# Splitting one unit's output product into three single-pass matmuls, with its conversion and a softmax step moved, in a chained attention and two-layer MLP kernel

## The chip, the cores and the metric

The kernel runs on one core of one Trainium2 chip. The metric is the device time of one execution in microseconds (us); the median of the runs shown is compared.

## The reference

A packed attention (32 packed queries `p` attend to `k`, `v`; then `q` attends to that packed result) gives an array of 2304 tokens by 512. It goes through two two-layer MLPs: the first with softplus, the second with SiLU (512 to 2048 to 512 each).

```python
p_packed = sm_attn(p, k, v)
out = sm_attn(q, p_packed, p_packed)
...
x = out.transpose(0, 2, 1, 3).reshape(B * S, H * D)
h = x @ w_in;  g = softplus(h);  x = g @ w_out
h = x @ w_in2; g = silu(h);      x = g @ w_out2
```

All data are float32 in size (the weights arrive as float64 words and are rebuilt on the chip).

## The kernel before, in words

**Products.** TensorE multiplies either plain float32 operands, or float32 operands that were split into a high and a low part of a type it takes in a single pass. A split product is three matmuls (low by high, high by low, high by high). Line 540 is the plain output product of the first MLP, line 547 the split one, line 501 its input product (always split; six matmuls for a chunk).

**Steps.** The first MLP and the attention are woven together by `run_steps` (line 767). A step s computes one chunk of 128 hidden features for one block of 288 tokens: the input product (`emit_in`), then softplus on ScalarE (`act_scalar`), and, for an earlier unit, one output column group dm of 128 (`emit_out`), which `finish_out` adds to or writes into the accumulator `ya`. A unit u is a set of chunks of one block. The first four units have two chunks each: u0 and u1 are chunks 0 and 1 of blocks 0 and 1 (steps 0 to 3), u2 and u3 are chunks 2 and 3 of blocks 0 and 1 (steps 4 to 7). From step 8 on a unit has four chunks (u4 is block 2, steps 8 to 11). The output products of u0 to u2 are issued two column groups at a time in steps 1 to 6; those of u3 one at a time in steps 8 to 11; step 7 has none. Before, u0 to u3 are all plain: softplus writes `gf` (line 507), and the product reads `wo_plain` (line 540). From u4 on softplus writes `gt` (513), ScalarE copies the high part `gh` (514), VectorE subtracts for the low part `gl` (`act_vector`, line 518), and line 547 multiplies.

**The order of the work is written out by hand** and every engine runs its own queue in that order. Attention pieces and weight conversions are generators (`Item`) which stop at named points: a step calls the points in the order next, D0, A0, input product, PE, `act_scalar`, `emit_out`, PE2, A1, D1, A2, `act_vector`, D, `finish_out`, D2. A generator due at the point that is called issues its next piece there. `OS` (line 763) gives for each early output weight the step of its high copy (line 176, at A0) and of its low subtraction (line 178, at D0).

**The attention pieces that lie in steps 4 to 11.** `att1(2)`: scores (330) at step 6, row maxima (336) at the end of step 6, exponentials `e0`, `e1` (342) in step 7, their transposes (351, `turn`) in step 9, copies out of PSUM (355, 358) in step 9, weighting with v (366) in step 10, normalising (391 to 394) at the end of step 10, a last transpose (399) in step 11 and its copy (403). `att2(3)` (block 3): product (414) and transpose (423) in step 5, row maxima (427, 428) at the end of step 6, exponential (430) in step 7, then "normalise" (432 to 439: sum, reciprocal, multiply, 32-square transpose) at D0 of step 8, high copy (444) and low part (446) of block 3's activations in step 8. Block 3 is first multiplied in step 12.

**Buffers.** PSUM results `h` and `y` have two banks each, the attention's `psa` two pairs. A bank is free for the product two further on only when its reader (softplus for h, `finish_out` for y) is done. `gh`/`gf` and `gl` have eight buffers each, `gt` two.

Of the kernel before, what the change touches and what calls it, by code (L numbers as in the profile page):

```python
# [18 lines left out]
B, H, S, D = 4, 8, 576, 64  # L19
# [31 lines left out]
def body(ctx, tc, kT, vv, qT, pT, wi1, wo1, wi2, wo2, out):  # L51
# [265 lines left out]
    def att1(b):  # L317

        HS = S // 2
        sm = l0.tile([P, 8], F32, name="sm", bufs=2)  # L320
        e, et, s1 = [None] * NR, [None] * NR, [None] * NR

        def scores():
            pz, kt = kts[b]
            s1[:] = two_banks(), two_banks()
            for half in range(2):
                for k in range(NK):
                    for r in range(NR):
                        rows = slice(64 * r, 64 * r + 64)
                        nc.tensor.matmul(  # L330
                            s1[r][32 * k:32 * k + 32, half, :HS], lhsT=pz[rows, k, :],
                            rhs=kt[rows, k, half * HS:(half + 1) * HS], start=True, stop=True,
                        )

        def top(r):
            nc.vector.tensor_reduce(
                out=sm[:, 2 + r:3 + r], in_=s1[r][:, :, :HS], axis=AX.XY, op=ALU.max, negate=True
            )

        def exp(r):  # L340
            e[r] = att.tile([P, S], F32, name=f"e{r}")
            nc.scalar.activation(  # L342
                out=e[r].rearrange("p (h s) -> p h s", h=2), in_=s1[r][:, :, :HS],
                func=AF.Exp, bias=sm[:, 2 + r:3 + r],
            )

        def turn(r):
            t = s1[r] = two_banks()
            for c in range(KC):
                n = min(P, S - c * P)  # L350
                nc.tensor.transpose(t[:n, c // 4, (c % 4) * P:(c % 4 + 1) * P], e[r][:, c * P:c * P + n], ident)

        def turned(r):
            et[r] = att.tile([P, KC, P], F32, name="et", bufs=2)
            nc.scalar.activation(
                out=et[r][:, :4, :], in_=s1[r][:, 0, :].rearrange("p (c f) -> p c f", c=4), func=AF.Copy
            )
            nc.scalar.activation(out=et[r][:64, 4, :], in_=s1[r][:64, 1, :P], func=AF.Copy)

        def weigh(*at):  # L360
            vt = vts[b]
            for r, c in at:
                n = min(P, S - c * P)
                for k in range(NK):
                    h = 2 * k + r
                    nc.tensor.matmul(  # L366
                        po[32 * k:32 * k + 32, r, :D1], lhsT=et[r][:n, c, 32 * k:32 * k + 32],
                        rhs=vt[:n, c, h * D1:(h + 1) * D1], start=(c == 0), stop=(c == KC - 1),
                    )

        yield "PE"
        scores()
        yield "D2" if b == 2 else "D"
        top(0)
        top(1)
        yield "A1"
        exp(0)
        exp(1)
        yield "PE"
        turn(0)  # L380
        turn(1)
        yield "A1"
        turned(0)
        turned(1)
        yield "PE2"

        po = two_banks()
        chunks = [(r, c) for r in range(NR) for c in range(KC)]
        weigh(*(sorted(chunks, key=lambda rc: rc[1] == KC - 1) if b else chunks))
        yield "D2"  # L390
        nc.vector.tensor_scalar(out=sm[:, 4:6], in0=po[:, :, D], scalar1=1e-9, scalar2=None, op0=ALU.add)
        nc.vector.reciprocal(out=sm[:, 6:8], in_=sm[:, 4:6])
        px = att.tile([P, NR, D], F32, name="px")
        nc.vector.tensor_tensor(
            out=px, in0=po[:, :, :D], in1=sm[:, 6:8].unsqueeze(2).to_broadcast([P, NR, D]), op=ALU.mult
        )
        yield "PE" if b == 1 else "PE2"
        pt_ps = two_banks()[:, 0, :P]
        nc.tensor.transpose(pt_ps, px.rearrange("p r d -> p (r d)"), ident)
        yield "A1"  # L400

        pt = pts[b] = l0.tile([P, P], F32, name="pt", bufs=B)
        nc.scalar.activation(out=pt, in_=pt_ps, func=AF.Copy)

    def att2(blk, last=False):

        b = blk // 2
        G = N0 // NP
        yield "PE"
        tq = two_banks()  # L410
        for k in range(NK):
            for r in range(NR):
                rows = slice(64 * r, 64 * r + 64)
                nc.tensor.matmul(  # L414
                    tq[32 * k:32 * k + 32, r, :N0], lhsT=pts[b][rows, k * NP:(k + 1) * NP], rhs=qts[blk][rows, k, :],
                    start=True, stop=True,
                )
        yield "D1"

        tr = att.tile([P, NR * G, NP], F32, name="tr", bufs=2)  # L420
        mx = att.tile([P, 2, NR * G], F32, name="mx", bufs=2)
        wide = [P, NR * G, NP]
        nc.vector.transpose(tr.rearrange("q (r g) p -> q r (g p)", r=NR), tq[:, :, :N0])
        if blk == 3:
            yield "next"
        yield "D2" if blk == 3 else "D"
        nc.vector.tensor_reduce(out=mx[:, 0], in_=tr, axis=AX.X, op=ALU.max)
        nc.vector.tensor_tensor(out=tr, in0=tr, in1=mx[:, 0].unsqueeze(2).to_broadcast(wide), op=ALU.subtract)
        yield "A1"
        nc.scalar.activation(out=tr, in_=tr, func=AF.Exp, scale=SCALE)  # L430
        yield "D" if blk == 2 else "D0"
        nc.vector.tensor_reduce(out=mx[:, 1], in_=tr, axis=AX.X, op=ALU.add)
        nc.vector.tensor_scalar(out=mx[:, 1], in0=mx[:, 1], scalar1=1e-9, scalar2=None, op0=ALU.add)
        nc.vector.reciprocal(out=mx[:, 1], in_=mx[:, 1])
        if blk == 2:
            yield "D2"
        nc.vector.tensor_tensor(out=tr, in0=tr, in1=mx[:, 1].unsqueeze(2).to_broadcast(wide), op=ALU.mult)
        tb = att.tile([P, NR, N0], F32, name="tb", bufs=1)
        nc.vector.transpose(tb, tr.rearrange("q (r g) p -> q r (g p)", r=NR))
        if last:  # L440
            yield "next"
        yield "A1"
        cols = slice(blk * N0, (blk + 1) * N0)
        nc.scalar.activation(out=ax[:, :NR, cols], in_=tb, func=AF.Copy)
        yield "D"
        nc.vector.tensor_tensor(
            out=ax[:, NR:, cols], in0=tb, in1=ax[:, :NR, cols].bitcast(F32), op=ALU.subtract
        )
# [53 lines left out]
        return h  # L502

    def act_scalar(s, h):
        if s < 2 * GJ:
            gf = g0.tile([P, N0], F32, name="gf", tag="gh")
            nc.scalar.activation(out=gf, in_=h, func=AF.Softplus)
            gs[steps[s]] = gf
            return None
        gt = cp.tile([P, N0], F32, name="gt")  # L510
        gh = g0.tile([P, N0], F32R, name="gh")
        gl = g0.tile([P, N0], F32R, name="gl")
        nc.scalar.activation(out=gt, in_=h, func=AF.Softplus)  # L513
        nc.scalar.activation(out=gh, in_=gt, func=AF.Copy)  # L514
        return gt, gh, gl
# [7 lines left out]
    def emit_out(s):  # L523
        u, i = steps[s]
        if s < 2 * GJ:
            if s not in AHEAD:
                return []
            u, first = AHEAD[s]
            dms = first, first + 1
        else:  # L530
            u, dms = u - 1, (i,)
        js, blk = units[u]
        n = BLOCKS[blk][1]
        ys = []
        for dm in dms:
            y = ps.tile([P, 512], F32, name="y")[:, :n]
            c = slice(dm * P, (dm + 1) * P)
            for x, j in enumerate(js):
                if len(js) < GJ:
                    nc.tensor.matmul(  # L540
                        y, lhsT=wo_plain[j][:, c], rhs=gs[u, x], start=(j == js[0]), stop=(j == js[-1])
                    )
                    continue
                gh, gl = gs[u, x]
                wh, wl = whl["o", j]
                for m, (w, g) in enumerate(((wl, gh), (wh, gl), (wh, gh))):
                    nc.tensor.matmul(  # L547
                        y, lhsT=w[:, c], rhs=g, start=(j == js[0] and m == 0), stop=(j == js[-1] and m == 2)
                    )
            ys.append((u, dm, y))  # L550
        return ys
# [152 lines left out]
    def start():  # L704
# [55 lines left out]
        for k, n, ss in ("i", 2, (1,)), ("i", 3, (2,)), ("o", 2, (3,)), ("o", 3, (4,)):  # L760
            plan(w[k, n], ss)

        OS = (3, 4), (4, 5), (5, 6), (10, 11)
        for n in range(GJ):
            plan(w["o", n], OS[n])

    def run_steps(end):
        for s in range(end):
# [19 lines left out]
            if s == 1:  # L788
                for y in ys:
                    finish_out(*y)  # L790
                    items[0].run("A1")
                ys = []
            go("A1")
            go("D1")
            go("A2")
# [633 lines left out]
```

## Time and profile before

| | us |
|---|---|
| median of 3 runs | 740.46 (740.44 to 740.78) |
| the profiled execution's own time | 740.1 |
| its span, first to last instruction | 738.3 |
| TensorE busy | 729.5 |
| VectorE busy | 564.1 |
| ScalarE busy | 388.9 |

Instructions are named by engine (PE is TensorE, PEld its weight loads, DVE VectorE, ACT ScalarE, POOL GpSimd, SP the queue that issues DMAs) and by line. A timeline row gives the start, the duration and the count of neighbouring like instructions; in brackets stands the idle time ahead of them and what ended it. Neighbours overlap a little, since a matmul's or an activation's tail runs under the next one; the spacing of starts is what one costs in a queue. A plain float32 matmul shows as two records.

### The profile page before, as it was taken

To read this page: it belongs to the slowest core of one execution; us is meant where nothing else is said; L and a number is where in the kernel's file an instruction comes from. 1 tells how busy PE (TensorE), PEld (TensorE's weight loads), DVE (VectorE), ACT (ScalarE), POOL (GpSimd) and SP (SyncE) were. 2 spreads that over 40 slices of the span, in tenths; PEclk is the share of its full clock that TensorE was granted. 3 is DMA by queue.
4 is the path that set the end of the run, shared out by engine and by line. 5 is a ranking of instruction groups with operands and counts; after the bars stand their busy time and mean duration, and the time that the engine had idled before them with its cause. 6 is when DMAs were issued, how large, how long until landed. Compare 5 with 4: busy or idle time off the path is not lost.

```text
span 738.3 us, 13860 instructions
## 1 busy us (share of the span) xinstructions
PE 729.5 (99%) x5402; PEld 698.0 (95%) x5402; DVE 564.1 (76%) x1017; ACT 388.9 (53%) x745; POOL 162.3 (22%) x140
## 2 busy tenths in 40 slices
PE   8999999999999999999999999999999999999997
PEld 7876999999999999999999999999999999999997
DVE  3888887879878897897746685767776976877667
ACT  3667886656555664566535544443353453454341
POOL 0000000000000000000000000000267999966755
PEclk9999999999999999999999999999999999999999
DMA  8965033145454362474359888789999789998942
GB/s 342 354 221 180 9 144 115 59 186 166 168 211 160 141 222 92 158 270 170 146 150 377 304 327 322 259 310 343 363 348 382 271 270 374 330 349 286 310 135 92
DMA packets 64674, 173.73 MB, mean 235 GB/s; under 512 B 5728, under 2 KB 34400, under 8 KB 61280
## 3 DMA queue, kind: packets, MB, share of 16 engines
q1 hardware_dynamic: 64608, 172.85, 65.5%
q8 instruction: 42, 0.69, 0.4%
q14 instruction: 24, 0.20, 0.1%
HBM read 136.65 MB, written 36.18 MB: 234 GB/s over the span
## 4 chain that ended last, share of the span: by engine, by line
PE 94%; ACT 3%; DVE 2%; issue 0%; POOL 0%; POOLq 0%; DVEq 0%
PE y L547 25%; PE y L1028 13%; PE h L501 13%; PE y L1140 11%; PE pA L970 7%; PE pC L970 7%; PE pB L970 7%; PE pD L970 3%; PE y L698 2%; PE psa L463 2%; PE y L540 2%; PE psa L330 1%; PE psa L366 1%; PE psa L414 1%; ACT e L342 0%
## 5 line engine op out<-in xcount | busy, mean ns | idle before, releaser
L547 PE MATMUL y<-gh,w 128*128 128x288 f32 x960 | 212.0, 296 | 0.1
L547 PEld LDWEIGHTS y<-gh,w 128*128 128x128 f32 x960 | 160.5, 188 | 12.8 <-issue 5.9
L547 PE MATMUL y<-gl,w 128*128 128x288 f32 x480 | 141.6, 295 | 0.0
L1002 POOL TENSOR_TENSOR sums<-c 128x384 f32<-128x384 f32 x13 | 15.5, 1193 | 500.6 <-ACT c L1292 500.6
L501 PE MATMUL h<-ax,vw 128*128 128x288 f32 x768 | 124.4, 297 | 0.0
L501 PEld LDWEIGHTS h<-ax,vw 128*128 128x128 f32 x768 | 108.9, 188 | 2.0 <-issue 0.5
L1028 PE MATMUL y<-G,w 128*128 128x384 f32 x480 | 93.8, 334 | 0.0
L547 PEld LDWEIGHTS y<-gl,w 128*128 128x128 f32 x480 | 90.1, 188 | 0.5 <-DVE gl L518 0.5
L1140 PE MATMUL y<-G,w 128*128 128x384 f32 x480 | 89.5, 334 | 0.0
L1028 PEld LDWEIGHTS y<-G,w 128*128 128x128 f32 x480 | 84.2, 188 | 0.0
L513 ACT ACTIVATE gt<-h 128x288 f32<-128x288 f32 x120 | 48.5, 405 | 67.0 <-PE h L501 62.3
L1140 PEld LDWEIGHTS y<-G,w 128*128 128x128 f32 x480 | 83.7, 188 | 0.0
L518 DVE TENSOR_TENSOR gl<-gt,gh 128x288 fp32r<-128x288 f32 x120 | 54.2, 452 | 25.2 <-ACT gh L514 24.4
L970 PE MATMUL pA<-xc,w 128*128 128x384 f32 x288 | 57.8, 335 | 0.1
L970 PE MATMUL pB<-xc,w 128*128 128x384 f32 x288 | 57.7, 334 | 0.0
L970 PE MATMUL pC<-xc,w 128*128 128x384 f32 x288 | 57.7, 334 | 0.0
L514 ACT ACTIVATE gh<-gt 128x288 fp32r<-128x288 f32 x120 | 53.4, 445 | 3.8
L1288 ACT ACTIVATE tc<-tc 128x384 f32<-128x384 f32 x24 | 12.6, 526 | 75.5 <-DVE tc L1188 75.4
L563 DVE TENSOR_TENSOR ya<-y,ya 128x288 f32<-128x288 f32 x104 | 46.9, 452 | 7.2 <-PE y L547 7.0
L970 PEld LDWEIGHTS pA<-xc,w 128*128 128x128 f32 x288 | 50.4, 188 | 0.4 <-ACT ta L1210 0.4
L970 PEld LDWEIGHTS pB<-xc,w 128*128 128x128 f32 x288 | 50.6, 188 | 0.0
L1010 POOL TENSOR_TENSOR G<-sums,G 128x384 fp32r<-128x384 f32 x40 | 49.0, 1248 | 7.1 <-ACT G L1006 7.1
(143 smaller groups left out, 1168.8 us busy)
## 6 DMA issues: line engine op xcount, KB each, us to landing
w<-wd SPq DMA_DIRECT2D x84, 512.0 KB, 5.9
wd<-whl SPq DMA_DIRECT2D x8, 1792.0 KB, 6.8
w<-td SPq DMA_DIRECT2D x56, 256.0 KB, 6.2
w<-od SPq DMA_DIRECT2D x42, 256.0 KB, 5.3
w<-od SPq DMA_DIRECT2D x20, 512.0 KB, 6.2
wraw<-wi SPq DMA_DIRECT2D x16, 512.0 KB, 5.6
wraw<-wo SPq DMA_DIRECT2D x16, 512.0 KB, 6.1
raw<-wi SPq DMA_DIRECT2D x16, 512.0 KB, 6.4
```

What stands on the lines that cost most here:

```text
L463: nc.tensor.matmul(t[32 * k:32 * k + 32, r, :512 if wide else 256], lhsT=pts[b][rows, k * NP:(k + 1) * NP], rhs=w[rows, :], start=True, st ...
L501: nc.tensor.matmul(h, lhsT=w, rhs=x, start=(i == 0), stop=(i == len(mm) - 1))
L513: nc.scalar.activation(out=gt, in_=h, func=AF.Softplus)
L514: nc.scalar.activation(out=gh, in_=gt, func=AF.Copy)
L518: nc.vector.tensor_tensor(out=gl, in0=gt, in1=gh.bitcast(F32), op=ALU.subtract)
L547: nc.tensor.matmul(y, lhsT=w[:, c], rhs=g, start=(j == js[0] and m == 0), stop=(j == js[-1] and m == 2))
L563: nc.vector.tensor_tensor(out=acc, in0=y, in1=acc, op=ALU.add)
L970: nc.tensor.matmul(out, lhsT=a, rhs=b, start=start and not i, stop=not start and i == len(mm) - 1, skip_group_check=True,)
L1002: eng.tensor_tensor(out=sum_of(q), in0=a, in1=b, op=op)
L1010: eng.tensor_tensor(out=u[:, 1], in0=sum_of(q), in1=u[:, 0].bitcast(F32), op=ALU.subtract)
L1028: nc.tensor.matmul(y, lhsT=w, rhs=g, start=not m, stop=m == len(mm) - 1)
L1140: nc.tensor.matmul(y, lhsT=a[:, c], rhs=G[:, g, h, j], start=(k % 2 == j == m == 0), stop=(k % 2 == j == 1 and m == 2),)
```

## The change

- The test for plain work becomes `u < 3` in place of "fewer than four chunks": u3 (block 1, chunks 2 and 3; steps 6 and 7) now writes `gt`, `gh`, `gl`, and its output products in steps 8 to 11 are split ones.
- Output weight 3 gets its high and low parts in steps 6 and 7 in place of 10 and 11.
- `att1(2)`'s transposes are issued at PE2 of step 9, behind that step's output product, in place of PE, ahead of it.
- `att2(3)`'s normalise is issued at D1 of step 7 in place of D0 of step 8.
- In step 8, `finish_out` is issued right behind PE2, ahead of A1, D1, A2 and `act_vector`.

```diff
@@ att1
-        yield "PE"
+        yield "PE2" if b == 2 else "PE"
         turn(0)
         turn(1)
@@ att2
-        yield "D" if blk == 2 else "D0"
+        yield "D" if blk == 2 else "D1" if blk == 3 else "D0"
         nc.vector.tensor_reduce(out=mx[:, 1], in_=tr, axis=AX.X, op=ALU.add)
@@ act_scalar
-        if s < 2 * GJ:
+        if steps[s][0] < 3:
             gf = g0.tile([P, N0], F32, name="gf", tag="gh")
@@ emit_out
-                if len(js) < GJ:
+                if u < 3:
                     nc.tensor.matmul(
                         y, lhsT=wo_plain[j][:, c], rhs=gs[u, x], start=(j == js[0]), stop=(j == js[-1])
                     )
@@ start
-        OS = (3, 4), (4, 5), (5, 6), (10, 11)
+        OS = (3, 4), (4, 5), (5, 6), (6, 7)
@@ run_steps
+            if s == 2 * GJ:
+                finish_out(*ys.pop())
             go("A1")
             go("D1")
             go("A2")
```

## Rows read from the trace of the kernel before

**Rows 1.** The page: its head, the granted clock of its slices, its chain by engine.

```profile
span 738.3 us, 13860 instructions
...
PEclk9999999999999999999999999999999999999999
...
PE 94%; ACT 3%; DVE 2%; issue 0%; POOL 0%; POOLq 0%; DVEq 0%
```

**Rows 2.** The chain that ended last: start, duration, what (0 to 90 us).

```profile
28.05 1.09 PE psa L351 x10
...
33.97 1.41 PE psa L366 x80
...
36.37 0.20 PE psa L399
36.58 0.60 PE psa L463 x16
...
40.11 0.65 PE psa L414 x16
...
49.68 2.14 PE y L540 x8
51.81 0.81 PE h L501 x6
...
52.65 0.41 ACT gf L507
...
62.57 0.46 DVE gl L518
...
70.33 0.67 PE psa L463 x16
```

**Rows 3.** Timeline of PE, steps 8 to 14 and one later step without attention work.

```profile
53.24 1.13 PE L540 MATMUL y<-gf,wraw 128*128 128x288 f32 x4
54.00 1.16 PE L501 MATMUL h<-ax,vw 128*128 128x288 f32 x6
55.82 1.43 PE L351 MATMUL psa<-ident,e 128*128 128x128 f32 x10 [0.66 <-ACT e L342]
...
60.42 1.24 PE L540 MATMUL y<-gf,wraw 128*128 128x288 f32 x4 [1.16 <-DVE ya L563]
...
64.89 1.04 PE L501 MATMUL h<-ax,vw 128*128 128x288 f32 x6
...
72.62 0.96 PE L501 MATMUL h<-ax,vw 128*128 128x288 f32 x6
...
99.94 0.30 PE L547 MATMUL y<-gh,w 128*128 128x288 f32 x1
...
101.52 0.96 PE L501 MATMUL h<-ax,vw 128*128 128x288 f32 x6
```

**Rows 4.** Timeline of DVE, steps 6 to 8.

```profile
50.55 0.65 DVE L178 TENSOR_TENSOR w<-wraw,w 128x512 fp32r<-128x512 f32 x1
51.38 0.76 DVE L446 TENSOR_TENSOR ax<-tb,ax 128x576 fp32r<-128x576 f32 x1 [0.18 <-ACT ax L444]
...
54.24 1.41 DVE L336 TENSOR_REDUCE sm<-psa 128x1 f32<-128x576 f32 x2
55.57 0.74 DVE L432 TENSOR_REDUCE mx<-tr 128x18 f32<-128x576 f32 x1
...
57.65 0.78 DVE L439 STREAM_TRANSPOSE tb<-tr 128x576 f32<-128x576 f32 x1
```

**Rows 5.** Timeline of ACT, steps 6 and 8.

```profile
50.66 0.68 ACT L444 ACTIVATE ax<-tb 128x576 fp32r<-128x576 f32 x1 [1.87 <-DVE tb L439]
...
58.18 0.45 ACT L514 ACTIVATE gh<-gt 128x288 fp32r<-128x288 f32 x1
```

**Rows 6.** Timeline of PE: the first matmuls, later ones of the same kind, the last.

```profile
1.34 5.49 PE L698 MATMUL y<-ident 128*128 128x128 f32 x24 [1.34 <-POOL ident masks.py:199]
...
16.40 3.39 PE L698 MATMUL y<-ident 128*128 128x128 f32 x28
...
733.66 0.68 PE L1028 MATMUL y<-tw,w 128*128 128x384 f32 x3
```

**Rows 7.** Windows behind the last matmul: busy time of PE, PEld, DVE, ACT, POOL, clock, DMA.

```profile
737.00:737.20 0.20, 0.00 (x0) 0.00 (x0) 0.00 (x0) 0.00 (x0) 0.00 (x0) 1.00 0.00 0
737.20:737.40 0.20, 0.00 (x0) 0.00 (x0) 0.00 (x0) 0.00 (x0) 0.00 (x0) 0.50 0.00 0
```

## The prediction

> **What bounds the kernel now.** I read the page first. Its chain of waits is PE for 94% of the span [rows 1], so in nearly all of the kernel a matmul saved is time saved, and a stall of PE in the early steps is carried to the end. All that the change touches lies between 47 and 68 us, so I went on to the chain there in order of time [rows 2], and it says something else: it leaves PE behind step 7's input product (the row at 51.81), runs over ACT from 52.65 and over DVE from 62.57, and comes back to PE only at 70.33. In steps 7 to 13 PE is not the bound.
>
> The timelines say where PE waits. In step 9 it waits 0.66 us for the exponentials, in step 10 it waits 1.16 us for a y bank that `finish_out` of step 8 has not freed [rows 3]. On DVE, steps 6 to 8 are one block of work with next to no holes: the low part of block 2 at 51.38 (0.18 idle ahead of it), accumulations, maxima, then the normalise of block 3 from 55.57 to 57.65 + 0.78 = 58.43 [rows 4].
>
> **The change, part by part.**
>
> *Split in place of plain products.* A column group of u3 is two products. Plain, eight records (four products) took 2.14 us, so one product is 0.535 us [rows 2]. Split, a step's twelve matmuls take 101.52 - 99.94 = 1.58 us, so one is 0.132 and a product of three 0.395 [rows 3]. Eight products save 8 x 0.14 = 1.1 us of PE.
>
> *What the split adds.* ACT gets two `gh` copies, 0.45 us each [rows 5]; DVE two `gl` subtractions, 0.46 each [rows 2]. In step 6, `gh` and the moved high copy of output weight 3 (some 0.6 us; I price it as its low half on DVE, 0.65 [rows 4]) go into ACT's 1.87 us of waiting ahead of the row at 50.66 [rows 5]: nothing. Were that cover gone, block 2's high copy would start up to 1.1 us later. In step 7, `gh` pushes ACT's exponentials back by up to 0.45; the transposes that read them are now behind more work, and it does not show. DVE's `gl` of step 6 fits partly into the 0.18 hole and pushes DVE by about 0.15 (bounds 0 and 0.46).
>
> *Weight 3's conversion in steps 6 and 7.* It issues no DMA, and no queue of SP or POOL is passed. Its low subtraction comes to lie at D0 of step 7, between the maxima and the normalise: 0.60 us by the spacing of starts, 0.65 busy [rows 4], all of it in DVE's solid block.
>
> *Normalise at D1 of step 7.* This is the term that decides. D1 comes ahead of `act_vector` in a step. Without a `gl` in step 7 the move would be nothing, since no DVE work lay between D1 of step 7 and D0 of step 8. With the split there is one: `gl` of step 7. It now queues behind the normalise, and the fifth of the six matmuls of step 8's output product reads it. Behind that matmul on PE stand the input products of steps 9, 10 and 11, all in order. So: normalise ends at 58.43 + 0.15 + 0.60 = 59.2; `gl` takes 0.46; the fifth matmul starts at about **59.65**. Step 8's first four matmuls would be done by 53.9 (start at about 53.4, as the row at 53.24, plus 4 x 0.132). PE stands idle for **about 5.7 us**, where the longest wait of these steps was 1.16.
>
> From there PE has no wait that I can find until step 14: two matmuls 0.26, then input product 0.80, output 0.79, transposes 1.09 (step 9), 0.80 + 0.79 + 1.41 (step 10), 0.80 + 0.79 + 0.20 (step 11) [rows 2, 3], 7.7 together: step 12 starts at 67.4, against 64.89 before [rows 3], 2.5 later. Steps 12 and 13 hold 2 x (0.80 + 0.65 + 0.60 + 1.58) = 7.3 us of work [rows 2, 3] and took 72.62 - 64.89 = 7.7 because DVE was late (the row at 70.33 [rows 2]); with DVE's low part of weight 3 gone from step 11 and PE later, that wait goes. Step 14 starts at 74.7 against 72.62: **+2.1 us** (bounds 1.7 and 2.5, for the 0.15 above and for waits of a few tenths). Behind it all producers are fed by PE itself and no wait of PE there is for a DMA, so it is carried to the end.
>
> *Transposes behind the output product, `finish_out` early.* Both remove waits (0.66 and 1.16 [rows 3]) that the longer one swallows; worth nothing here. `finish_out` of step 8 now stands ahead of `gl` of step 8 and of block 3's low part and waits for the stalled product itself; what is queued behind it is wanted only in steps 10 to 12. If the stall were not there, the 1.16 would go.
>
> *The clock.* The granted clock is full in every slice of the page [rows 1]. But the trace shows twice what PE does about idleness. After the last matmul (733.66 + 0.68 = 734.34 [rows 6]) the clock falls from 1.00 to 0.50 at 737.2 [rows 7], so 2.9 us later. And at the start, out of idleness, 24 matmuls take 5.49 us, 229 ns each, where 28 of the same kind later take 121 ns each [rows 6]: some 5.4 us at half rate, 1.2 GHz, which lost 24 x 0.108 = 2.6 us. A wait of 5.7 us is twice those 2.9, so I take it that the clock falls in it, and that the work behind it (PE alone is then the bound) runs at half rate for a while. Bounds: zero, by the waits of 1.16 that left the clock full, and 2.6 by the start. I take 2.2: near the start's row, and under it because that engine had done nothing at all before.
>
> The Trainium skill, TensorE: Matmul & The Clock Gate, section "What's actually happening", says the half rate is the default and activity releases it; the two rows agree. By that rule the sum is +4.3; by the full clock of the page's slices alone it would be +2.1.
>
> *The sum.* 2.1 + 2.2 = **+4.3 us**. The profiled execution took 740.1; the median of runs is 0.36 above it. So 744.4 for a profile and **744.8** for the median.
>
> **The rivals.**
>
> *The stall without the clock.* PE stands for 5.7 us, but the clock stays or comes back at once. For it: no early wait moved it. Against: rows 7. 740.46 + 2.1 = 742.6, still 0.28% slower. Chance 0.16.
>
> *The stall isn't there; no change.* This needs `gl` of step 7 to run ahead of the normalise, say because the point D1 is reached a step later than I read it. Then `gl` is done at about 55.57 + 0.15 + 0.60 + 0.46 = 56.8, PE's wait is some 2.9 us, as much as the work that it then has in hand: step 9 starts at 57.1, and 7.5 us of work put step 12 at 64.6, plus a few tenths of waits for a later exponential chain, against 64.89. DVE's chain to 70.33 stays, and the time stays within a few tenths of 740.5. It decides from the point at which `gl` is done before about 57. Against it: the order of points in `run_steps`. Chance 0.07.
>
> *Faster.* DVE's queue runs ahead of what I laid out, so that the early `finish_out` and the later transposes take away 0.66 + 1.16 and the split its 1.1: 2.9 us at most, 737.6. Against it: DVE's maxima alone reach to 55.65 [rows 4], and ACT's chain holds steps 8 to 10 [rows 2]. Chance 0.05.
>
> **How the numbers follow.** The stall with the clock has 0.72 and gives 744.8. The range takes in the rival without the clock: from 1.7 + 0 above the median (742.2) to 2.5 + 2.6 above it, and 0.34 for the scatter of the runs shown, 746.0 rounded up. About 0.2% (1.5 us) is what a measurement of this kernel tells from no change. Slower: 0.72 + 0.16 = 0.88; same 0.07; faster 0.05.
>
> **What would show it.** In the profile after: a row of DVE with the normalise and `gl` of line 518 behind it, near 59; a wait of PE at line 547 on `gl` of over 5 us, in place of 0.66 and 1.16; a granted clock under 1.00 in the windows near 58 to 65, with input products of 1.6 us rather than 0.8; step 12 near 69 to 70. Wrong if `gl` of step 7 ends before 57, if PE's wait is under 3 us, or if step 14's start moved by less than 1.5 us. If the clock stays at 1.00 throughout, the second term falls and the first stands.

## The result, and the profile after

The changed kernel takes **744.94 us** (median of 4 runs, 744.52 to 746.15) against 740.45 (4 runs, 740.41 to 740.78): the ratio is 1.0054, 95% interval 1.0036 to 1.0072, so it is slower by some half a per cent (the two medians are 4.5 us, 0.6%, apart). Its profiled execution took 744.98. One execution of a later run took 2528 us where its eleven others took 740.94 to 745.37, and it is left out below.

The page of the kernel after, its head and the granted clock of its 40 slices:

```profile
span 743.2 us, 13882 instructions
...
PEclk9998999999999999999999999999999999999999
```

Where every slice was full before [rows 1], the fourth (55.7 to 74.3 us) now is not. The timeline of PE after, steps 8 to 14:

```profile
53.77 0.29 PE L547 MATMUL y<-gh,w 128*128 128x288 f32 x1
56.77 0.37 PE L547 MATMUL y<-gh,w 128*128 128x288 f32 x1 [2.70 <-DVE w L178]
59.79 0.61 PE L547 MATMUL y<-gl,w 128*128 128x288 f32 x1 [2.66 <-DVE gl L518]
...
60.44 1.64 PE L501 MATMUL h<-ax,vw 128*128 128x288 f32 x6
61.88 0.44 PE L547 MATMUL y<-gh,w 128*128 128x288 f32 x1
...
63.32 1.56 PE L351 MATMUL psa<-ident,e 128*128 128x128 f32 x10
...
69.52 1.04 PE L501 MATMUL h<-ax,vw 128*128 128x288 f32 x6
...
76.93 0.96 PE L501 MATMUL h<-ax,vw 128*128 128x288 f32 x6
77.82 1.80 PE L330 MATMUL psa<-kt,pz 64*32 64x288 f32 x32
```

The rows answer to [rows 3]. Step 8's output product stops twice: its fourth matmul waits 2.70 us for the low half of weight 3, its fifth 2.66 us for step 7's `gl`. The two waits of before (0.66 in step 9, 1.16 in step 10) are gone. Step 9's input product then takes 61.88 - 60.44 = 1.44 us, where it takes 0.8 at the full clock. Step 12 starts at 69.52 (64.89 before), step 14 at 76.93 (72.62 before).

The timeline of DVE after, answering to [rows 4]:

```profile
55.94 0.68 DVE L178 TENSOR_TENSOR w<-wraw,w 128x512 fp32r<-128x512 f32 x1
56.54 0.74 DVE L432 TENSOR_REDUCE mx<-tr 128x18 f32<-128x576 f32 x1
...
58.62 0.78 DVE L439 STREAM_TRANSPOSE tb<-tr 128x576 f32<-128x576 f32 x1
59.32 0.41 DVE L518 TENSOR_TENSOR gl<-gt,gh 128x288 fp32r<-128x288 f32 x1
```

The order is as the step's points say: weight 3's low half (L178), the normalise (L432 to L439), and only then `gl` of step 7 (L518) at 59.32. Its operand `gh` had been ready since 53.81 (ScalarE's line 514, 0.45 us from 53.36), so it was the queue that held it. PE's fifth matmul starts at 59.79. The timeline of ACT, answering to [rows 5]:

```profile
50.93 0.69 ACT L444 ACTIVATE ax<-tb 128x576 fp32r<-128x576 f32 x1 [0.87 <-DVE tb L439]
```

ACT's wait ahead of block 2's high copy shrank from 1.87 to 0.87 us and took in the extra copies; the row's start moved from 50.66 to 50.93, and 0.27 of that is a shift from ahead of the change: everything from 15 us on lies some 0.28 us later in this execution, where PE waits 0.23 us for the load of the first q block.

The clock, in windows of 1 us (columns as in [rows 7]: length, then busy time and count of PE, PEld, DVE, ACT and POOL, then the clock, the DMA share and GB/s):

```profile
56.00:57.00 1.00, 0.23 (x1) 0.19 (x1) 1.00 (x3) 1.00 (x2) 0.00 (x0) 1.00 0.00 0
57.00:58.00 1.00, 0.14 (x1) 0.00 (x0) 0.90 (x4) 0.98 (x2) 0.00 (x0) 0.56 0.00 0
60.00:61.00 1.00, 1.00 (x5) 1.00 (x6) 0.32 (x1) 0.12 (x1) 0.00 (x0) 0.50 0.00 0
63.00:64.00 1.00, 1.00 (x7) 0.98 (x6) 0.90 (x2) 0.01 (x1) 0.00 (x0) 0.53 0.00 0
64.00:65.00 1.00, 1.00 (x11) 1.00 (x10) 0.01 (x1) 0.63 (x2) 0.00 (x0) 1.00 0.00 0
```

It falls to 0.50 just after 57.0 us, with PE idle but for one matmul since 54, and is back at 1.00 shortly before 64.

### The profile page after: what moved, and what is told of

It is laid out like the page before. It is cut to its first block, busy times and chain, and to the rows that moved or that the text cites. A ratio compares the mean times of both kernels' runs of the same rounds, so it can differ in the third digit from the quotient of the medians.

```text
span 743.2 us, 13882 instructions
## 1 busy us (share of the span) xinstructions
PE 730.7 (98%) x5410; PEld 700.8 (94%) x5410; DVE 565.0 (76%) x1019; ACT 390.1 (52%) x747; POOL 162.5 (22%) x140
## 4 chain that ended last, share of the span: by engine, by line
PE 93%; DVE 2%; ACT 2%; DMA 1%; SPq 1%; issue 0%; DVEq 0%
PE y L547 26%; PE h L501 13%; PE y L1030 13%; PE y L1142 11%; PE pA L972 7%; PE pC L972 7%; PE pB L972 7%; PE pD L972 3%; PE psa L463 2%; DMA qt<-qT 1%; PE y L540 1%; PE y L698 1%; PE psa L414 1%; PE psa L366 1%; PE psa L330 0%
## 5 line engine op out<-in xcount | busy, mean ns | idle before, releaser
L547 PE MATMUL y<-gh,w 128*128 128x288 f32 x976 | 217.2, 297 | 2.8 <-DVE w L178 2.7
L547 PEld LDWEIGHTS y<-gh,w 128*128 128x128 f32 x976 | 163.9, 188 | 15.7 <-issue 5.9
L547 PE MATMUL y<-gl,w 128*128 128x288 f32 x488 | 144.6, 296 | 2.7 <-DVE gl L518 2.7
L547 PEld LDWEIGHTS y<-gl,w 128*128 128x128 f32 x488 | 92.0, 189 | 3.4 <-DVE gl L518 3.4
L518 DVE TENSOR_TENSOR gl<-gt,gh 128x288 fp32r<-128x288 f32 x122 | 55.1, 452 | 27.1 <-ACT gh L514 26.2
```

The costliest lines, as they stand in the source:

```text
L518: nc.vector.tensor_tensor(out=gl, in0=gt, in1=gh.bitcast(F32), op=ALU.subtract)
L547: nc.tensor.matmul(y, lhsT=w[:, c], rhs=g, start=(j == js[0] and m == 0), stop=(j == js[-1] and m == 2))
```

## The experiments

Nine kernels, each timed in five rounds beside the kernel before on the same chip.

### One line undone: the normalise back at D0

```diff
-        yield "D" if blk == 2 else "D1" if blk == 3 else "D0"
+        yield "D" if blk == 2 else "D0"
```

> The changed kernel with one line undone: block 3's normalise is back at D0 of step 8, so that step 7's low subtraction runs ahead of it. My theory (the normalise ahead of that subtraction is what holds PE): the fifth matmul of step 8's output product starts near 57.0 us instead of 59.8, the fourth still waits for weight 3's low half to 56.8, PE waits some 2.9 us in one piece or two, and the rest of the gain is eaten by VectorE's chain in steps 11 to 13: 740.6 us (740.2 to 741.0) with the clock at 1.00. If 2.9 us of waiting is enough for the clock to fall in some executions, those are 1 to 2 us longer. Rival (the stall comes from the conversion of weight 3 or from the added copies, not from the normalise): 743 us or more.

Measured: 742.3 us (median of 12, 740.87 to 742.85) against 740.7, ratio 1.0017 (1.0008 to 1.0025). The profiled execution is the shortest, 740.87. Its PE and DVE timelines:

```profile
56.91 0.37 PE L547 MATMUL y<-gh,w 128*128 128x288 f32 x1 [2.70 <-DVE w L178]
57.18 0.41 PE L547 MATMUL y<-gl,w 128*128 128x288 f32 x1
...
57.56 0.96 PE L501 MATMUL h<-ax,vw 128*128 128x288 f32 x6
...
65.24 1.04 PE L501 MATMUL h<-ax,vw 128*128 128x288 f32 x6
```

```profile
56.68 0.45 DVE L518 TENSOR_TENSOR gl<-gt,gh 128x288 fp32r<-128x288 f32 x1
57.05 0.74 DVE L432 TENSOR_REDUCE mx<-tr 128x18 f32<-128x576 f32 x1
```

`gl` of step 7 now runs ahead of the normalise (56.68, then L432 at 57.05), the fifth matmul starts at 57.18, and step 12 at 65.24, within 0.4 us of before [rows 3]. So 59.79 - 57.18 = 2.6 us of PE's stall in the changed kernel hang on this one line; what is left is the wait for weight 3's low half. The median is 1.7 us above what I expected of a full clock: the profiled execution alone has a mean clock of 1.000, the eleven others 0.995 to 0.998. Of the kernel before, one execution in the 24 beside them is under 0.999 (0.998).

### The same, with PE kept busy

```diff
+            if s == 2 * GJ:
+                warm(11)
             ys = emit_out(s) if ys is None else ys
```

(`warm` is the kernel's own helper, line 694; the edit is made to the kernel of the last run.)

> The kernel with the normalise put back to D0 of step 8 (the run norm_back), and 11 matmuls of the identity by itself (22 records, some 2.7 us, read by nobody) on PE ahead of step 8's output product. My theory: the 1.4 us by which most executions of norm_back are longer than its profiled one are the clock, falling in the 2.7 us of waiting; filled, every execution has the clock at 1.00 (0.999 or more as a mean) and takes 740.9 us (740.6 to 741.3). Rival (the scatter has another cause, such as transfers): the median stays near 742.3 us.

Measured: 740.67 us (740.29 to 741.96) against 740.65, ratio 1.0002 (0.9993 to 1.0010); every execution has a mean clock of 0.999 or more. More work on PE, and 1.6 us less: what made most executions of the last run longer was the clock, lowered where the wait of 2.7 us stood unfilled. None of those lower ones was traced, so where in them the clock fell is not shown.

### The changed kernel with its stall filled

```diff
+            if s == 2 * GJ:
+                warm(22)
             ys = emit_out(s) if ys is None else ys
```

> The changed kernel with 22 matmuls of the identity by itself (44 records, 121 ns each at full rate, 5.3 us, into a y bank that nobody reads) issued on PE ahead of step 8's output product. It does more work, and the order on VectorE and ScalarE is that of the changed kernel. My theory (the idle PE lets the clock fall, and the half rate behind the wait costs about 2.1 us): the fifth matmul still starts near 59.8, the granted clock stays 1.00 throughout, the input product of step 9 takes 0.8 us instead of 1.44, and the time is 742.8 us (742.4 to 743.2). Rival (the slow matmuls behind the wait have another cause, or the wait alone costs it all): 744.9 us or more.

Measured: 743.33 us (742.91 to 743.40) against 740.7, ratio 1.0030 (1.0019 to 1.0041). Timeline of PE, and windows:

```profile
53.63 5.07 PE L698 MATMUL y<-ident 128*128 128x128 f32 x44
...
59.91 0.40 PE L547 MATMUL y<-gl,w 128*128 128x288 f32 x1 [0.68 <-DVE gl L518]
...
60.28 0.95 PE L501 MATMUL h<-ax,vw 128*128 128x288 f32 x6
61.07 0.30 PE L547 MATMUL y<-gh,w 128*128 128x288 f32 x1
...
67.76 1.05 PE L501 MATMUL h<-ax,vw 128*128 128x288 f32 x6
...
75.17 0.96 PE L501 MATMUL h<-ax,vw 128*128 128x288 f32 x6
```

```profile
60.00:64.00 4.00, 4.00 (x32) 4.00 (x33) 2.32 (x5) 2.48 (x8) 0.00 (x0) 1.00 0.00 0
```

The fifth matmul starts at 59.91, as in the changed kernel, so VectorE's queue is untouched; the clock stays at 1.00, step 9's input product takes 61.07 - 60.28 = 0.79, step 12 starts at 67.76 instead of 69.52, and step 14 at 75.17 instead of 76.93. The time, 2.6 us above before, is 0.1 us above the window that I gave, and the loss is 1.9 us smaller than the changed kernel's 4.5. This separates the two terms: 2.6 for the stall, 1.9 for the clock.

### Weight 3 one step earlier

```diff
-        OS = (3, 4), (4, 5), (5, 6), (6, 7)
+        OS = (3, 4), (4, 5), (5, 6), (5, 6)
```

> The changed kernel with weight 3's conversion one step earlier still (high half in step 5, low half at D0 of step 6). My theory (the fifth matmul, not the fourth, decides): the fourth no longer waits, the fifth starts at the same 59.6 to 59.9, since VectorE has the same work ahead of step 7's low subtraction; the time is that of the changed kernel, 744.9 us (744.5 to 745.8). Rival (the wait for weight 3's low half is a second part of the cost): 742.2 us, the first 2.7 us of waiting gone.

Measured: 746.28 us (745.54 to 749.37) against 740.7, ratio 1.0075 (1.0058 to 1.0092).

```profile
48.90 1.94 PE L330 MATMUL psa<-kt,pz 64*32 64x288 f32 x32
50.77 2.21 PE L540 MATMUL y<-gf,wraw 128*128 128x288 f32 x8
...
54.95 0.43 PE L547 MATMUL y<-gh,w 128*128 128x288 f32 x2
60.68 0.61 PE L547 MATMUL y<-gl,w 128*128 128x288 f32 x1 [5.31 <-DVE gl L518]
```

The fourth matmul no longer waits, and the fifth waits 5.31 us in one piece: the wait for weight 3 was only the front half of the wait for `gl`, as I expected, and the rival is out. What I had not expected is 1.3 us more. Step 6's output product starts at 50.77 (49.61 before, the chain's row at 49.68 [rows 2]), step 8's at 54.69 (53.24 [rows 3]), 1.45 later; 0.64 of it is this run's own shift at 15 us. So some 0.8 us went by moving the conversion into steps 5 and 6. The trace shows where 0.5 of it went. ScalarE now has two high copies in step 5 (line 176, 1.14 us from 44.31), and its next copy out of PSUM (line 471) starts at 47.65, where the changed kernel's starts at 46.76; 0.37 of these 0.89 us is the difference of the two runs' shifts. VectorE's line 479 needs that copy, and step 6's scores wait for line 479: 1.94 us from 48.90, against 1.43 before.

### Everything but the split

The two tests of the split go back to those of before; the rest of the change stays.

```diff
-        if steps[s][0] < 3:
+        if s < 2 * GJ:
...
-                if u < 3:
+                if len(js) < GJ:
```

> The changed kernel without its split: u3's products stay plain, all else (weight 3 in steps 6 and 7, transposes behind the output product, normalise at D1, accumulation early in step 8) is kept. My theory: without a low subtraction in step 7 the normalise at D1 delays nothing, the bank wait of 1.16 us in step 10 goes, and VectorE's chain to step 13 gives back most of it: 740.2 us (739.9 to 740.5), so at most 0.05% faster than before. Rival (the other edits are worth the waits that they remove, 1.2 to 1.8 us): 738.7 to 739.3 us.

Measured: 740.25 us (739.86 to 740.71) against 740.7, ratio 0.9991 (0.9982 to 1.0000).

```profile
58.77 1.06 PE L501 MATMUL h<-ax,vw 128*128 128x288 f32 x6 [0.96 <-ACT gt L513]
59.99 1.24 PE L540 MATMUL y<-gf,wraw 128*128 128x288 f32 x4 [0.16 <-DVE ya L563]
61.78 1.50 PE L366 MATMUL psa<-vt,et 128*32 128x65 f32 x80 [0.55 <-ACT et L358]
...
70.33 0.67 PE L463 MATMUL psa<-wraw,pt 64*32 64x256 f32 x16
```

Without a `gl` in step 7 the normalise at D1 delays nothing. The bank wait of step 10 falls from 1.16 to 0.16, but step 10 now waits 0.96 for the softplus of step 8 and 0.55 for the copies of the transposes, and the attention product of step 13 starts at 70.33, as before [rows 2], in an execution that lay 0.44 us later at step 4 (39.38 against 38.94). The other edits remove 1.8 us of waits and find ScalarE's and VectorE's behind them; some 0.4 came through, as the expectation had it.

### The three low subtractions on GpSimd

```diff
-        nc.vector.tensor_tensor(out=gl, in0=gt, in1=gh.bitcast(F32), op=ALU.subtract)
+        eng = nc.gpsimd if s < 2 * GJ else nc.vector
+        eng.tensor_tensor(out=gl, in0=gt, in1=gh.bitcast(F32), op=ALU.subtract)
...
-        nc.vector.tensor_tensor(out=lo, in0=y, in1=hi.bitcast(F32), op=ALU.subtract)
+        eng = nc.gpsimd if (k, n) == ("o", 3) else nc.vector
+        eng.tensor_tensor(out=lo, in0=y, in1=hi.bitcast(F32), op=ALU.subtract)
```

> The changed kernel, all its edits kept (the normalise at D1 too), but the low subtractions of steps 6 and 7 and that of weight 3 run on GpSimd, which has next to nothing to do there, in place of VectorE. My theory (the place behind the normalise in VectorE's queue is the whole cost): step 7's low part is ready near 55, the wait at the fifth matmul falls under 1 us, the clock stays at 1.00, PE's 1.1 us of saved products and the removed waits come through since VectorE has 1.5 us less to do: 739.5 us (739.1 to 740.2), faster than both kernels. Rival (ScalarE's chain of exponentials and table loads, or a GpSimd that is slower beside VectorE, holds PE anyway): 740.5 us or more.

Measured: 740.85 us (740.20 to 742.84) against 740.65, ratio 1.0006 (0.9997 to 1.0014). Timelines of PE, POOL, DVE and ACT:

```profile
54.59 0.40 PE L549 MATMUL y<-gl,w 128*128 128x288 f32 x1
...
59.29 1.06 PE L502 MATMUL h<-ax,vw 128*128 128x288 f32 x6 [0.96 <-ACT gt L514]
...
64.91 1.04 PE L502 MATMUL h<-ax,vw 128*128 128x288 f32 x6
```

```profile
50.74 1.74 POOL L179 TENSOR_TENSOR w<-wraw,w 128x512 fp32r<-128x512 f32 x1
53.72 0.81 POOL L520 TENSOR_TENSOR gl<-gt,gh 128x288 fp32r<-128x288 f32 x1 [1.25 <-ACT gh L515]
```

```profile
51.48 1.61 DVE L447 TENSOR_TENSOR ax<-tb,ax 128x576 fp32r<-128x576 f32 x1 [0.15 <-ACT ax L445]
```

```profile
55.44 0.69 ACT L431 ACTIVATE tr<-tr 128x576 f32<-128x576 f32 x1 [0.49 <-DVE tr L429]
```

The changed kernel with all its edits, the normalise at D1 among them, loses its stall by the engine of three subtractions, two of which PE had waited for: weight 3's low half and `gl` of step 7. The latter is done at 54.5 and the fifth matmul starts at 54.59. So it was their place in VectorE's queue. But the gain that I hoped for did not come: step 10 waits 0.96 us for softplus, and step 12 starts at 64.91, where it started before. A part of it is that VectorE got slower: the subtraction of L447 (446 in the kernel before) takes 1.61 us beside a GpSimd subtraction of 1.74, where it took 0.76 [rows 4], and ScalarE's first exponential then waits 0.49 us for VectorE. That is not the whole of it: the run with everything but the split has the same wait of 0.96 without a subtraction on GpSimd. The rival held. The Trainium skill, GPSIMD Engine Reference, section "1. Specifications", says that GpSimd shares its SBUF interfaces with VectorE and contends with VectorE instructions that have two SBUF inputs; that subtraction has two, and these rows agree.

### Another conversion taken out of VectorE's queue

From the kernel before, without a split: the accumulation of step 8 early, and input weight 4 converted later.

```diff
-        for n, s in (("i", 4), 11), (("i", 5), 19), (("i", 6), 26), (("i", 7), 28):
+        for n, s in (("i", 4), 23), (("i", 5), 19), (("i", 6), 26), (("i", 7), 28):
...
+            if s == 2 * GJ:
+                finish_out(*ys.pop())
             go("A1")
```

> The kernel before with two edits: step 8's accumulation early, as the change has it, and input weight 4's conversion (two ScalarE and three VectorE instructions, some 1.9 us of VectorE) at steps 23 and 24 in place of 11 and 12; it is first read in step 30. No split. My theory (in steps 11 to 13 VectorE's queue is the bound, so that a wait removed ahead of it gives nothing unless VectorE is relieved): 739.7 us (739.4 to 740.1). Rival (PE or ScalarE is the bound there): 740.3 us or more.

Measured: 740.3 us (739.96 to 741.08) against 740.65, ratio 0.9994 (0.9983 to 1.0005).

```profile
69.94 0.64 PE L463 MATMUL psa<-wraw,pt 64*32 64x256 f32 x16
...
72.19 0.96 PE L501 MATMUL h<-ax,vw 128*128 128x288 f32 x6
73.09 1.79 PE L330 MATMUL psa<-kt,pz 64*32 64x288 f32 x32
```

```profile
105.61 0.69 DVE L164 SCALAR_TENSOR_TENSOR wraw<-wraw,wx 128x512 int32<-128x512 int32 x1
106.22 0.45 DVE L518 TENSOR_TENSOR gl<-gt,gh 128x288 fp32r<-128x288 f32 x1
```

```profile
106.73 0.40 PE L547 MATMUL y<-gl,w 128*128 128x288 f32 x1 [0.47 <-DVE gl L518]
```

The wait of step 13 is gone (the attention product starts at 69.94), step 14 starts 0.43 us earlier than before in spite of a start that was 0.59 us later at 15 us: 1.0 gained. Step 14's scores then give 0.3 back (1.79 us from 73.09, against 1.47 in the same place before), and near 106 us the conversion's last instruction at 105.61 makes the next `gl` late (106.22; before it ran at 104.44), for which PE waits 0.47. Moving the work moved the wait. The median is the rival's 740.3, but not for the rival's reason: the wait ahead of step 13 went as my theory had it, and the gain was lost behind it.

> Both of the two: the changed kernel with its three low subtractions on GpSimd, and input weight 4's conversion at steps 23 and 24. My theory: with VectorE relieved by the first, it is no longer the bound in steps 11 to 13, so that the second adds next to nothing: 739.5 us (739.0 to 740.1), the same as with GpSimd alone within 0.3 us. Rival (the two gains add): 738.7 us.

Both together: 741.13 us (740.94 to 745.37) against 740.65, ratio 1.0016 (1.0003 to 1.0029). No gain, and by the medians a loss of 0.5 us. The profile shows a loss of each of the two runs again, 0.96 us of waiting for softplus in step 10 and 0.47 us for a late `gl` near 107 us; I did not follow the rest.

With the conversion at steps 27 and 28:

```diff
-        for n, s in (("i", 4), 23), (("i", 5), 19), (("i", 6), 26), (("i", 7), 28):
+        for n, s in (("i", 4), 27), (("i", 5), 19), (("i", 6), 26), (("i", 7), 28):
```

> The run plain_later with input weight 4's conversion at steps 27 and 28 in place of 23 and 24, where the windows of the kernel before show VectorE least busy (2.23 of 4 us); it is first read in step 30. My theory: plain_later gained about 1 us by step 14 and lost 0.33 there and some 0.7 near 106 us, where its moved conversion made the low part of step 24 late; at step 27 the second loss goes, 739.7 us (739.3 to 740.1), faster than both kernels by 0.1%. Rival (VectorE has no room there either, or the loss near 106 us has another cause): 740.3 us, as plain_later.

Measured: **739.8 us** (739.32 to 741.41) against 740.76, ratio 0.9984 (0.9976 to 0.9993). It is faster than the kernel before by 0.16%, as I expected, and so also than the changed kernel (744.94, timed on another occasion), by 0.7%; and it has no split in u3 at all. In its trace `gl` near 106 us starts at 105.93, ahead of the moved conversion, and PE does not wait for it, so the second loss is gone; step 14's scores still take 1.79.

## Why the prediction was right

It said 744.8 us in a range of 742.2 to 746.0, slower with 0.88; measured were 744.94. The terms, one by one:

- **The saved products, the copies, the conversion in ScalarE's cover.** As forecast: ScalarE's wait of 1.87 took the copies in and kept 0.87, and a split output product of u3 takes 0.80 us at the full clock (61.07 to 61.87 in the filled run), against 0.79. The 0.60 that I took for weight 3's low half does not follow from rows 4, which give 0.65; the changed kernel's spacing (55.94 to 56.54) is 0.60.
- **`gl` behind the normalise.** The fifth matmul was forecast at 59.65 and came at 59.79, of which 0.27 is the shift from ahead of the change. Putting the normalise back brought it to 57.18, taking `gl` off VectorE to 54.59. One thing I had wrong: I let the first four matmuls run freely, but the fourth reads weight 3's low half, which stands in the same queue just ahead of the normalise. It cost nothing of its own (the run with weight 3 earlier has one wait of 5.31). But it cut the wait in two, 2.70 and 2.66. So the wait on `gl` of over 5 us that was to show me right did not appear as one, and each piece is under the 3 us that were to show me wrong. I had the length of the stall right, not its make-up.
- **The stall's price, forecast 2.1 (1.7 to 2.5).** With the clock kept up, the kernel is 2.6 us above before by its runs. In that profile, step 12 starts 67.76 - 64.89 = 2.87 late, of which 0.39 is that run's own shift at 15 us: 2.5, as forecast. Step 14 starts 75.17 - 72.62 = 2.55 late, less the 0.39: 2.16, against 2.1. Missing from my sum are some tenths behind step 14: 0.33 at step 14's scores (1.80 us from 77.82 in the changed kernel, 1.47 before), which wait 0.5 us for VectorE's line 479 there.
- **The clock's price, forecast 2.2 (0 to 2.6).** PE worked at half rate from 59.79 to about 63.9 in the changed kernel's profile, which loses half of 4.15 us: 2.1. Filling the stall gave back 1.9 (filling the shorter wait of the kernel with the normalise put back, 1.6). The clock fell just after 57.0 us, behind the first of the two waits, so that it fell before PE had stood for the 5.7 us from which I argued. And one row under the 2.2 says less than I took from it: the start's matmuls are twice as long as later ones [rows 6], but in the same trace the granted clock reads 1.00 from 1 to 7 us, so their half rate is inferred from their lengths alone.
- **The sum.** 4.5 measured, 4.3 forecast. Step 14 moved by 4.31, less the 0.27 of the start 4.0, against 4.3: the stall's 2.16 is as forecast, the clock's 1.9 is 0.3 under, and the tenths behind step 14, which I had not counted, made it up. That the sum came out within 0.2 is in part luck.
- **The rival without the clock** is the run with the stall filled: forecast 742.6, measured 743.3. **The rival without the stall** is the run with the normalise put back: forecast within a few tenths of 740.5, measured 742.3. That price was wrong by the clock alone, since with its wait filled the same kernel took 740.67. I had let the clock fall only for the wait of 5.7 us; with one of 2.7 the mean clock was lower in eleven of twelve executions.
- **The move of the normalise alone** was priced at nothing. In a kernel that has only this edit, each engine's instructions stand in the same order as before, so it was not run; that too is argued from the order of the points alone.

## What to carry to other kernels

An engine's queue is in order, so a new instruction can cost what stands ahead of it and not only its own duration: 0.46 us of work behind 2.8 us of normalise held the bound engine for 2.7 us more. A move that changes nothing alone can decide everything beside another edit, so lay the queue out with all edits in it, and ask for each new operand which matmul reads it first. And price a long wait of TensorE twice, once as idle time and once as the half-rate work behind it: some matmuls that nobody reads took back 1.6 to 1.9 us here.

## What the runs showed that I had not expected

- With a PE wait of 2.70 us the mean clock was lower (0.995 to 0.998) in 11 of 12 executions, and 1.000 in the profiled one; with the wait filled it was lower in none of 11. The kernel before has such executions too, 5 of the 76 beside all these runs.
- At the start of the kernel the clock can fall as well. In the profiled execution of the last kernel it is at half in this stretch (windows of that kernel, columns as above):

```profile
13.00:14.60 1.60, 0.59 (x29) 0.36 (x18) 1.18 (x5) 0.67 (x1) 0.00 (x0) 1.00 1.02 413
14.70:18.00 3.30, 3.30 (x35) 2.56 (x42) 1.30 (x3) 0.77 (x2) 0.00 (x0) 0.50 1.04 401
```

  That execution took 741.41 us, the other eleven 739.32 to 740.25; just ahead of the stretch PE had waited 1.01 us (line 399, for VectorE). At the same place the kernel before waits 0.90 and the changed kernel 0.94, and their clock stays full there. Why it fell in the one and not in the others was not tried.
- VectorE's two-input subtraction took 1.61 us in place of 0.76 while GpSimd subtracted beside it. A VectorE reduction with one input (line 428, at 53.74) took 0.74 us beside GpSimd's next subtraction, as it does in the kernel before.
